# Query planes laid out to meet the high keys twice, fewer transfers per pair of heads, and a reordered start, in a fused attention and gated-MLP kernel

## The chip, the cores and the metric

One core of one Trainium2 chip. The metric is the device time of one execution in microseconds (us), as the median of several runs. Engines: PE (TensorE), DVE (VectorE), ACT (ScalarE), POOL (GpSimd) and SP (SyncE, which here only issues transfers).

## The reference

Windowed attention with a few sink keys, then a two-matrix network with a gate; all in float32, the weights come as float64. In short:

```python
# q, k, v: (4, 8, 768, 64); n_sink = 4, window = 128
scores = scale * np.matmul(q, k.transpose(0, 1, 3, 2))
keep = is_sink | in_window            # key < 4, or 0 <= row - key < 128
a = softmax(np.where(keep, scores, -1e9))
x = (a @ v) with heads side by side   # (4, 768, 512)
h = np.maximum(x @ w_in, 0.0)         # w_in (512, 1024)
conv = sum(conv_w[k] * shifted(h, k - 1) for k in range(3))   # along the rows
out = (h * sigmoid(conv)) @ w_out     # w_out (1024, 512)
```

## The kernel before

**Tiling.** Two heads share the 128 rows of the chip's memories: head 0 of a pair in rows 0 to 63, head 1 in rows 64 to 127. There are 16 pairs (four per batch), numbered g. A pair has six query tiles of 128; a tile meets its own 128 keys, the 128 before, and the 4 sinks (`KW` = 132 columns per key tile, the last 4 a copy of the sinks). One *step* is one query tile of one pair; `banded` (L451) walks 96 steps, 24 per batch, and fills the PE's time between them with pieces of the MLP of earlier rows (`Moe.unit`, L180). All engines run their own queues in program order; a scheduler that builds the program orders each queue by priorities and its own idea of time, and semaphores join them.

**Batch 0** (`prep32`, L349) scores in plain float32: q and k are transposed on PE (L357), ACT evacuates them (L288), q once per head with the other head's rows multiplied by zero (`headscale`).

**Batches 1 to 3** (`prep`, L295) split every float32 into a high and a low part of a shorter format and need three products: high q with high k, low q with high k, high q with low k. `turn_k` (L316) transposes a half of k, ACT casts it to two planes of `kk` (L334), DVE makes the low part in a scratch tile `bk` (L337), SP moves that to planes 2 and 3 (L340), ACT spreads the sinks over all four planes (L342), and two more transfers copy each head's high keys into the other head's rows (L344, L345). The other halves of planes 2 and 3 are zero; the first use of each `kk` copies them from a zeroed tile (L326). `turn_q` (L302) transposes, evacuates to scratch `bq` (ACT L288, DVE L310), and four transfers per half put high q in a head's own rows and low q in the other head's rows of `X` (L313, L314). `scores` (L372) then makes two products per head: X with plane j (high q on high k, low q on high k: L381), X with plane 2 + j (high q on low k, low q on zeros: L382). That is 8 + 4 + 2 transfers of this kind per pair, beside two loads each of q and k and one of v.

**The start.** SP loads the first halves of q and k of pairs 0 and 1 (L871), a flag is computed from `n_sink` and `window` (L874 to L876), and all engines branch on it (L906). After the branch DVE builds the mask tiles `w1`, `w2` (L473 to L478) and their minima `m1`, `m2` (`narrow_masks`, L489), POOL zeroes `A.zeros` and `c.vs` (the sink values of batch 0, in a spare part of `kks`), SP loads v of pair 0, the first weight tile, and the raw q and k of pair 2 into the slots that pair 0's transposes free.

**Weights.** Sixteen tiles of float64 and one of conv taps are converted, one per step from step 2 on (`WHEN`): ACT one pass (L118), DVE three and a subtraction (L121, L122, L123, L131), POOL one (L130).

**Sinks of later batches** (`sink_fetch`, `sink_split`) are loaded at the first step of a batch and split 3 steps later, by ACT and DVE on 12 rows (L440 to L443), then moved to `vsr` by four transfers (L446, L448).

Of the kernel before, what the change touches and what calls it, by code (L numbers as in the profile page):

```python
# [10 lines left out]
F32 = mybir.dt.float32  # L11
# [24 lines left out]
AHEAD = 200  # L36

# [236 lines left out]
class Attn:  # L274


    def __init__(self, c, x, kw, mp, mps):
# [6 lines left out]
        self.zeros = None  # L284
# [4 lines left out]

    def pieces_of(self, name, dtype):  # L290

        both = self.mp.tile([P, 512, 2], dtype, tag="nat", name=f"b{name}", bufs=3).rearrange("p n w -> p (n w)")
        return [both[:, 3 * P * x:3 * P * x + 3 * P].rearrange("p (t k) -> p t k", t=3) for x in range(2)]

    def prep(self, g, s, ahead=lambda: None):  # L295
# [6 lines left out]
        def turn_q(half):  # L302
# [4 lines left out]
            X = s.X[half] = ap.tile([P, 2, HTL, P], F32R, tag="X", name=f"X{g}{half}", bufs=3)  # L307
            H, L = self.pieces_of(f"q{g}{half}", F32R)
            self.evac(H, pt, -1.0 / math.sqrt(D))
            c.emptied = [nc.vector.scalar_tensor_tensor(out=L, in0=pt, scalar=-1.0 / math.sqrt(D), in1=f(H), op0=ALU.mult, op1=ALU.subtract)]  # L310
            for j in range(2):
                r, o = (slice(D * x, D * x + D) for x in (j, 1 - j))
                nc.sync.dma_start(f(X[r, j]), f(H[r]))  # L313
                nc.sync.dma_start(f(X[o, j]), f(L[r]))  # L314

        def turn_k(half):  # L316
            if half == 0:
                if g % 2 not in self.KK:
                    self.KK[g % 2] = ap.tile([P, 4, T, kw], F32R, tag="kk", name=f"kk{g}")
                    for j in range(2):  # L320
                        r = slice(D - D * j, P - D * j)
                        plane = f(self.KK[g % 2][r, 2 + j]).rearrange("p t k -> p (t k)")
                        if self.zeros is None:
                            nc.gpsimd.memset(plane, 0.0)
                        else:
                            nc.sync.dma_start(plane, self.zeros[r])  # L326
                s.kk = self.KK[g % 2]
            kk = s.kk[:, :, HTL * half:HTL * half + HTL, 0:P]
# [4 lines left out]
            for j in range(2):  # L333
                nc.scalar.copy(kk[:, j], pt)  # L334
            if half == 0:
                s.low = self.pieces_of(f"k{g}", F32R)
            c.emptied = [nc.vector.tensor_tensor(out=s.low[half], in0=pt, in1=f(kk[:, 0]), op=ALU.subtract)]  # L337
            for j in range(2):
                r = slice(D * j, D * j + D)
# [602 lines left out]
```

## Time and profile before

| what | us |
|---|---|
| median of 3 runs | 474.92 (474.6 to 476.47) |
| the profiled execution, its own time | 473.48 |
| its span, first to last instruction | 471.8 |
| PE busy | 444.6 (94%) |
| DVE busy | 339.0 (72%) |
| ACT busy | 321.3 (68%) |
| POOL busy | 281.3 (60%) |
| span before the first transpose on PE | 6.9 |

A busy share is a mean over stages with different limits, and a PE instruction counts from its issue to its end though the next one overlaps it. So the stages are read one by one: the start, the first batch with the conversion of the weights (to about 90 us), the change from batch 0 to batch 1 (about 104 to 126 us), and the long rest.

### The profile page before, as it was taken

What the parts mean: (1) busy time and instruction counts of PE and PEld (TensorE: products, weight loads), DVE (VectorE), ACT (ScalarE), POOL (GpSimd) and SP (SyncE); (2) the same over time, 40 slices, a digit from 0 to 9 for tenths busy, and PEclk for the clock granted to TensorE, in tenths of its full rate; (3) what the DMA queues carried; (4) which work ended last, traced back from release to release, by engine and by line L of the source; (5) the groups of instructions that cost most, each with busy time, mean ns of one, the idle gap of its engine ahead of it and who ended that gap; (6) DMA issues with size and microseconds to landing.
All of it is one profiled execution on the core that took longest, in us unless ns stands there. A gap on an engine that the chain in (4) does not pass through costs nothing.

```text
span 471.8 us, 10560 instructions
## 1 busy us (share of the span) xinstructions
PE 444.6 (94%) x3181; PEld 388.3 (82%) x3181; DVE 339.0 (72%) x1190; ACT 321.3 (68%) x1027; POOL 281.3 (60%) x557
## 2 busy tenths in 40 slices
PE   3898989898899999999999999999999999999994
PEld 3576768697798988898989898988989898998982
DVE  4799999758858668786766859685767663665562
ACT  4989957768867868785867767675857654554542
POOL 3474786626858658676755757667656671445340
PEclk9999999999999999999999999999999999999998
DMA  6888674388667472655273655545250101000001
GB/s 140 219 229 251 183 201 107 81 199 203 167 153 179 137 175 68 161 146 133 61 192 81 166 119 134 143 120 124 71 141 15 46 1 46 0 23 24 24 24 53
DMA packets 105851, 55.91 MB, mean 119 GB/s; under 512 B 83072, under 2 KB 98712, under 8 KB 105784
## 3 DMA queue, kind: packets, MB, share of 16 engines
q1 hardware_dynamic: 105640, 55.00, 45.5%
q8 instruction: 28, 0.46, 0.4%
q14 instruction: 39, 0.32, 0.2%
q10 hardware_dynamic: 144, 0.13, 0.1%
HBM read 28.17 MB, written 6.29 MB: 73 GB/s over the span
## 4 chain that ended last, share of the span: by engine, by line
PE 75%; DVE 11%; ACT 4%; POOL 3%; DMA 2%; issue 2%; DVEq 0%; POOLq 0%; ACTq 0%
PE ph L204 26%; PE po L239 25%; PE px L655 7%; PE sc L382 3%; PE sc L381 3%; PE pts L617 3%; PE px L678 2%; DVE stm L122 2%; PE tq L305 1%; PE tk L331 1%; DVE stm L123 1%; DMA kk<-bk 1%; DMA raw<-in_q_dram 1%; DVE roomH L577 1%; DVE roomL L577 1%
## 5 line engine op out<-in xcount | busy, mean ns | idle before, releaser
L239 PE MATMUL po<-woH,g 128*128 128x512 f32 x384 | 138.2, 405 | 1.5 <-POOL g L226 0.8
L204 PE MATMUL ph<-xH,wiH 128*128 128x258 f32 (+1 forms) x384 | 110.7, 288 | 0.0
L204 PE MATMUL ph<-xL,wiH 128*128 128x258 f32 (+1 forms) x384 | 109.6, 286 | 0.0
L204 PE MATMUL ph<-xH,wiL 128*128 128x258 f32 (+1 forms) x384 | 109.1, 284 | 0.0
L226 POOL TENSOR_SCALAR g<-t 128x256 fp32r<-128x256 f32 x94 | 44.3, 472 | 74.5 <-DVE t L219 50.6
L586 POOL TENSOR_SCALAR pe<-pe,sm 128x132 f32<-128x132 f32 (+1 forms) x144 | 62.8, 447 | 37.7 <-DVE sm L584 19.2
L239 PEld LDWEIGHTS po<-woH,g 128*128 128x128 f32 x384 | 69.4, 189 | 13.2 <-POOL g L226 1.7
L227 POOL TENSOR_TENSOR g<-t,g 128x256 fp32r<-128x256 f32 x94 | 74.5, 793 | 5.8
L239 PE MATMUL po<-woL,g 128*128 128x512 f32 x192 | 76.1, 396 | 0.0
L216 DVE SCALAR_TENSOR_TENSOR t<-hb,cw,t 128x256 f32<-128x256 f32 x96 | 53.8, 560 | 29.4 <-ACT t L215 28.9
L204 PEld LDWEIGHTS ph<-xH,wiL 128*128 128x128 f32 x384 | 72.8, 190 | 2.2
L204 PEld LDWEIGHTS ph<-xH,wiH 128*128 128x128 f32 x384 | 72.7, 189 | 2.0
L204 PEld LDWEIGHTS ph<-xL,wiH 128*128 128x128 f32 x384 | 72.7, 189 | 1.6
L580 ACT ACTIVATE pe<-pe,sm 128x132 f32<-128x132 f32 (+1 forms) x144 | 58.2, 406 | 14.4 <-DVE sm L577 12.8
L218 ACT ACTIVATE t<-t 128x256 f32<-128x256 f32 x96 | 40.1, 418 | 36.3 <-DVE t L217 35.9
L219 DVE SCALAR_TENSOR_TENSOR t<-t,hb 128x256 f32<-128x256 f32 x96 | 48.3, 504 | 15.1 <-ACT t L218 14.3
L215 ACT ACTIVATE t<-hb,cw 128x256 f32<-128x256 f32 x96 | 49.0, 511 | 12.4 <-POOL g L227 10.1
L217 DVE SCALAR_TENSOR_TENSOR t<-hb,cw,t 128x256 f32<-128x256 f32 x96 | 54.4, 567 | 4.0 <-POOL pe L586 0.5
L211 ACT ACTIVATE hb<-ph 128x258 f32<-128x258 f32 (+1 forms) x96 | 36.8, 384 | 17.4 <-PE ph L204 13.9
L577 DVE CUSTOM_DVE_ANT_0 pe<-sc,m 128x132 f32<-128x132 f32 (+1 forms) x144 | 39.8, 287 | 7.7 <-PE sc L382 6.9
L381 PE MATMUL sc<-kk,X 128*128 128x260 f32 (+1 forms) x144 | 42.3, 304 | 1.5 <-issue 1.1
L655 PE MATMUL px<-pT,vraw 128*64 128x128 f32 (+1 forms) x512 | 43.0, 317 | 0.0
(161 smaller groups left out, 896.1 us busy)
## 6 DMA issues: line engine op xcount, KB each, us to landing
X<-bq SPq DMA_DIRECT2D x96, 96.0 KB
vraw<-in_v_dram SPq DMA_DIRECT2D x16, 384.0 KB
out_dram<-stm SPq DMA_DIRECT2D x23, 256.0 KB
kk<-kk SPq DMA_DIRECT2D x24, 198.0 KB
raw<-in_k_dram SPq DMA_DIRECT2D x24, 192.0 KB
raw<-in_q_dram SPq DMA_DIRECT2D x24, 192.0 KB
kk<-bk SPq DMA_DIRECT2D x48, 96.0 KB
raw<-in_q_dram SPq DMA_DIRECT2D x16, 96.0 KB
```

Source lines behind the costliest of these rows:

```text
L204: self.latest = nc.tensor.matmul(u.h[:, 0:W], w[:, cc, ff * P:(ff + 1) * P], x[:, cc, t0:t1], start=(i == 0), stop=(i == len(prods) - 1))
L215: nc.scalar.mul(a, prev, cw[:, 0, ff:ff + 1])
L216: nc.vector.scalar_tensor_tensor(out=e, in0=this, scalar=cw[:, 1, ff:ff + 1], in1=a, op0=ALU.mult, op1=ALU.add)
L217: nc.vector.scalar_tensor_tensor(out=a, in0=nxt, scalar=cw[:, 2, ff:ff + 1], in1=e, op0=ALU.mult, op1=ALU.add)
L219: nc.vector.scalar_tensor_tensor(out=a, in0=e, scalar=1.0, in1=this, op0=ALU.add, op1=ALU.mult)
L227: nc.gpsimd.tensor_tensor(out=u.g[:, 1], in0=a, in1=f(u.g[:, 0]), op=ALU.subtract)
L239: ins = nc.tensor.matmul(po[:, 0:c.DM], u.g[:, a, tt * P:(tt + 1) * P], w[:, ff, :], start=(ff == 0 and i == 0), stop=(ff == NFF - 1 and i ...
L381: self.c.pin(self.nc.tensor.matmul(pc, X[:, j, u, :], kk[:, j, lo:hi], start=True, stop=False))
L577: nc.vector.tensor_tensor_reduce(out=pe[:, j, cols], in0=pc[:, P - at:SW][:, cols], in1=mk, op0=ALU.add, op1=ALU.min, scale=1.0, scalar=3. ...
L580: exp = nc.scalar.activation(pe[:, j, cols], pe[:, j, cols], AF.Exp, bias=sm[:, j:j + 1], scale=-1.0, accum_out=sm[:, 2 + 2 * j:3 + 2 * j])
L586: nc.gpsimd.tensor_scalar(pe[:, j, cols], pe[:, j, cols], sm[:, 8 + j:9 + j], 1.0, ALU.mult, ALU.mult)
L655: ins = nc.tensor.matmul(px[h][D * j:D * j + D, P * at:P * at + n], s.v[:, j, kt, :], pT, start=(h not in open_), stop=False, skip_group_c ...
```

## The change

- **q.** `X` has four planes. ACT evacuates q twice per half with `headscale`, so plane j holds high q of head j in its own rows and zeros in the other's; DVE makes plane 2 + j, the low part, zero in the other's rows. Then one transfer per head copies high q into the other head's rows of plane j.
- **k.** `kk` has two planes. The low part goes to a scratch tile `low`; after the second half one transfer per head moves it into the other head's rows of plane j. ACT spreads the sinks over two planes after the first half, POOL spreads them over `low`. No zero planes are left.
- **Products.** High q on both halves of the rows meets high keys in one half and low keys in the other; low q meets the same plane. Still two products per head and tile. Per pair 4 + 2 transfers stay of 14.
- **Start.** k of pairs 0 and 1 is loaded by ACT's queue; v of pair 0 before the branch. PE makes 8 products of zeros before the branch (`WAKE`), one after pair 0's q transposes and 3 after its k transposes (`IDLE`). One of the two evacuations of pair 0's q moves from ACT to DVE; the masks wait for it, their minima for step 21. The zeroed tiles and the batch 0 sink values live elsewhere.
- **Sinks** of batch 1 are fetched at step 21 instead of 24, and split at 24.

```diff
+WAKE = 8
+IDLE = {"q": 1, "k": 3}
         def turn_q(half):
...
-            H, L = self.pieces_of(f"q{g}{half}", F32R)
-            self.evac(H, pt, -1.0 / math.sqrt(D))
-            c.emptied = [nc.vector.scalar_tensor_tensor(out=L, in0=pt, scalar=-1.0 / math.sqrt(D), in1=f(H), op0=ALU.mult, op1=ALU.subtract)]
+            X = s.X[half] = ap.tile([P, 4, HTL, P], F32R, tag="X", name=f"X{g}{half}", bufs=3)
+            c.emptied = []
+            for j in range(2):
+                self.evac(X[:, j], pt, c.headscale[:, j:j + 1])
+                c.emptied.append(nc.vector.scalar_tensor_tensor(out=X[:, 2 + j], in0=pt, scalar=c.headscale[:, j:j + 1], in1=f(X[:, j]),
+                                                                op0=ALU.mult, op1=ALU.subtract))
             for j in range(2):
                 r, o = (slice(D * x, D * x + D) for x in (j, 1 - j))
-                nc.sync.dma_start(f(X[r, j]), f(H[r]))
-                nc.sync.dma_start(f(X[o, j]), f(L[r]))
+                nc.sync.dma_start(f(X[o, j]), f(X[r, j]))
         def turn_k(half):
...
-                nc.sync.dma_start(f(kk[r, 2 + j]), f(s.low[half][r]))
-            if half and kw > P:
-                nc.scalar.copy(s.kk[:, :, :, P:kw], f(s.kk[:, :, 0:1, 0:kw - P]).to_broadcast([P, 4, T, kw - P]))
+            if half == 0 and kw > P:
+                nc.scalar.copy(s.kk[:, :, :, P:kw], f(s.kk[:, :, 0:1, 0:kw - P]).to_broadcast([P, 2, T, kw - P]))
+                nc.gpsimd.tensor_copy(s.low[:, :, P:kw], f(s.low[:, 0:1, 0:kw - P]).to_broadcast([P, T, kw - P]))
             if half:
-                nc.sync.dma_start(f(s.kk[D:P, 0]), f(s.kk[0:D, 0]))
-                nc.sync.dma_start(f(s.kk[0:D, 1]), f(s.kk[D:P, 1]))
+                for j in range(2):
+                    r, o = (slice(D * x, D * x + D) for x in (j, 1 - j))
+                    nc.sync.dma_start(f(s.kk[o, j]), f(s.low[r]))
@@ prep32, pair 0 only
+                    ins = nc.tensor.matmul(c.spare, still[:, 0:P], still[:, 0:P], start=True, stop=True)
+                    if g == half == 0 and j:
+                        c.moved = nc.vector.tensor_scalar(s.X[half][:, j], pt, c.headscale[:, j:j + 1], None, ALU.mult)
@@ scores
-            self.c.pin(self.nc.tensor.matmul(pc, X[:, j, u, :], kk[:, 2 + j, lo:hi], start=False, stop=True))
+            self.c.pin(self.nc.tensor.matmul(pc, X[:, 2 + j, u, :], kk[:, j, lo:hi], start=False, stop=True))
@@ banded
-            nc.vector.tensor_tensor(out=mk[:, NS:KW], in0=w[:, 0:P], in1=w[:, KW:SW], op=ALU.min)
+            ins = nc.vector.tensor_tensor(out=mk[:, NS:KW], in0=w[:, 0:P], in1=w[:, KW:SW], op=ALU.min)
+            follow(c, ins, c.turned, "late")
...
+    follow(c, nc.vector.tensor_scalar(w1[:, KW:SW], inw, -NEG, NEG, ALU.mult, ALU.add), c.moved, "masks later")
...
-            if t == 0 and g and g % NPAIR == 0:
-                sinks = sink_fetch(c, m, g // NPAIR)
+            if i == NSTB - 3 or t == 0 and g > NPAIR and g % NPAIR == 0:
+                sinks = sink_fetch(c, m, max(1, g // NPAIR))
@@ attention_gated_mlp
+        for i in range(WAKE):
+            nc.tensor.matmul(turn, still[:, 0:P], still, start=True, stop=True)
     for i in range(RAWB):
-        load_half(c, i // 2, "qk"[i % 2], 0, c.raw[i])
+        load_half(c, i // 2, "qk"[i % 2], 0, c.raw[i], nc.scalar if i % 2 else nc.sync)
+    load_v(c, 0, 0, 0, T // 2)
```

How it moves instructions, at three places. First SP's queue behind the branch, before (`raw_67` and `raw_68` are the slots for raw q and k, `vraw_69` and `vraw_70` those for v, `wi_0r` the first weight tile):

```order
L401 DMA vraw_69<-in_v_dram 128x3x64 x2
L106 DMA wi_0r<-in_moe_w_in_dram 128x1024
L401 DMA raw_67<-in_q_dram 128x3x64 x2
L401 DMA raw_67<-in_k_dram 128x3x64 x2
L106 DMA wi_1r<-in_moe_w_in_dram 128x1024
L401 DMA raw_68<-in_q_dram 128x3x64
```

and now:

```order
L108 DMA wi_0r<-in_moe_w_in_dram 128x1024
L108 DMA wi_1r<-in_moe_w_in_dram 128x1024
L400 DMA raw_67<-in_q_dram 128x3x64 x2
L400 DMA vraw_70<-in_v_dram 128x3x64
L400 DMA raw_67<-in_k_dram 128x3x64 x2
L108 DMA wi_2r<-in_moe_w_in_dram 128x1024
```

The first two weight tiles now stand ahead of the third pair's q, one tile did before. Second, DVE's queue from the branch to the first weight tile, before (`m_147` is the mask of a first tile, `roomH` and `roomL` hold masks and scores of batch 0, `sc` are scores in the accumulators, `sm` row minima):

```order
L475 TENSOR_TENSOR roomH<-vraw_70 128x4
L471 TENSOR_SCALAR m_147<-m_147 128x128
L489 TENSOR_TENSOR m_148<-roomH 128x128
L476 TENSOR_SCALAR roomH<-roomH 128x4
L477 COPY roomH<-roomH 128x260
L478 TENSOR_SCALAR roomH<-vraw_70 128x4
L489 TENSOR_TENSOR m_149<-roomH 128x128
L577 ISA roomH,sm_163<-sc_0_0_208,m_147 128x128
```

and now:

```order
L472 TENSOR_SCALAR m_163<-m_163 128x128
L357 TENSOR_SCALAR X_192<-trq_187,headscale 128x384
L706 TENSOR_SCALAR roomL<-vraw_70 128x128
L707 TENSOR_SCALAR roomL<-vraw_70 128x128
L708 TENSOR_TENSOR roomL<-vraw_70 128x4
L709 TENSOR_SCALAR roomL<-roomL 128x4
L710 COPY roomL<-roomL 128x260
L711 TENSOR_SCALAR roomL<-vraw_70 128x4
L570 ISA roomH,sm_172<-sc_0_0_228,m_163 128x128
```

The evacuation of q stands ahead of the masks, and the two minima have gone from here. Third, SP's queue for the second pair of batch 1, before (`kk_1392` are its keys, `X_1470` and `X_1528` its two halves of q, `kk_1140` the keys of the pair after):

```order
L326 DMA kk_1392<-roomH 64x792 x2
L398 DMA vraw_70<-in_v_dram 128x12x64
L340 DMA kk_1392<-bk_1401 64x3x128 x4
L401 DMA raw_68<-in_q_dram 128x6x64
L313 DMA X_1470<-bq_1471 64x384
L314 DMA X_1470<-bq_1471 64x384
L313 DMA X_1470<-bq_1471 64x384
L314 DMA X_1470<-bq_1471 64x384
L344 DMA kk_1392<-kk_1392 64x792
L345 DMA kk_1392<-kk_1392 64x792
L313 DMA X_1528<-bq_1529 64x384 x2
L314 DMA X_1528<-bq_1529 64x384 x2
```

and now:

```order
L334 DMA kk_1413<-low_1414 64x792 x2
L397 DMA vraw_70<-in_v_dram 128x12x64
L311 DMA X_1486<-X_1486 64x384
L400 DMA raw_68<-in_q_dram 128x6x64
L311 DMA X_1486<-X_1486 64x384
L400 DMA raw_68<-in_q_dram 128x6x64
L311 DMA X_1543<-X_1543 64x384
```

Sixteen transfers of keys and queries stood there, six do now (the last one behind these rows); the four transfers into `vsr` (batch 1's sinks), which stood behind them, now stand ahead.

## Rows read from the trace of the kernel before

**Rows 1.** The page's chain that ended last, by engine.

```profile
PE 75%; DVE 11%; ACT 4%; POOL 3%; DMA 2%; issue 2%; DVEq 0%; POOLq 0%; ACTq 0%
```

**Rows 2.** Busy time by stage: window, its length, then PE, PEld, DVE, ACT, POOL, clock, DMA.

```profile
7.00:15.00 8.00, 7.03 (x25) 5.49 (x26) 3.90 (x22) 5.71 (x17) 3.43 (x11) 1.00 0.87 222
25.00:90.00 65.00, 57.82 (x432) 46.75 (x431) 62.98 (x182) 51.03 (x153) 43.25 (x62) 1.00 0.64 174
90.00:110.00 20.00, 20.00 (x175) 18.26 (x174) 12.81 (x50) 15.48 (x49) 7.23 (x15) 1.00 0.85 203
110.00:126.00 16.00, 13.07 (x87) 11.10 (x87) 13.24 (x64) 12.50 (x49) 12.94 (x26) 1.00 0.63 163
160.00:400.00 240.00, 239.70 (x1760) 213.00 (x1759) 171.74 (x652) 166.97 (x564) 156.72 (x320) 1.00 0.43 107
```

**Rows 3.** Timeline of the start: start, length, engine, line, what, idle before and its releaser.

```profile
6.91 0.88 PE L357 MATMUL trq<-ident,raw 128*128 128x128 f32 x3 [6.91 <-SPq L938]
...
7.68 0.42 SPq L106 DMA_DIRECT2D wi_0r<-in_moe_w_in_dram  x1
...
7.90 1.05 ACT L288 ACTIVATE X<-trq,headscale 128x384 f32<-128x384 f32 x2 [1.93 <-DVE roomH L474]
...
8.27 0.90 SPq L401 DMA_DIRECT2D raw<-in_q_dram  x2
...
9.01 0.90 PE L357 MATMUL trq<-ident,raw 128*128 128x128 f32 x3 [0.59 <-ACT X L288]
...
10.71 0.29 DVE L577 CUSTOM_DVE_ANT_0 roomH<-sc,m 128x128 f32<-128x128 f32 x1 [1.60 <-PE sc L378]
...
12.89 0.66 ACT L118 ACTIVATE stm<-wi_0r 128x512 f32<-128x512 f32 x1 [0.48 <-DMA wi_0r<-in_moe_w_in_dram]
...
13.60 0.88 PE L357 MATMUL trq<-ident,raw 128*128 128x128 f32 x3 [0.38 <-DMA kks<-in_v_dram]
...
13.69 0.41 DVE L121 TENSOR_SCALAR stm<-stm 128x512 int32<-128x512 int32 x1
...
15.44 0.49 PE L357 MATMUL trk<-ident,raw 128*128 128x128 f32 x3
...
15.67 0.69 DVE L122 SCALAR_TENSOR_TENSOR stm<-wi_0r,stm 128x512 int32<-128x512 int32 x1
```

**Rows 4.** Chain of waits in order of time, at the start.

```profile
8.27 4.86 DMA raw<-in_q_dram
```

**Rows 5.** Timeline of the change from batch 0 to batch 1: SP, PE, ACT, DVE.

```profile
106.18 3.02 SPq L340 DMA_DIRECT2D kk<-bk  x4
...
113.81 2.44 SPq L313 DMA_DIRECT2D X<-bq  x2
...
111.75 0.26 PE L637 MATMUL tk<-identr,sk 128*72 128x128 f32 x1 [0.67 <-DVE sk L629]
...
116.84 0.30 PE L381 MATMUL sc<-kk,X 128*128 128x128 f32 x1 [1.05 <-issue]
...
122.69 0.36 PE L381 MATMUL sc<-kk,X 128*128 128x260 f32 x1 [0.40 <-PE sc L382]
...
123.97 0.41 PE L617 MATMUL pts<-ident,pe 128*128 128x128 f32 x2 [0.80 <-ACT pT L619]
...
123.28 0.27 ACT L342 CAST kk<-kk 128x96 fp32r<-128x96 f32 x1 [1.60 <-DMA kk<-bk]
...
109.58 0.67 DVE L441 TENSOR_TENSOR sink<-sink 12x512 fp32r<-12x512 f32 x1
```

**Rows 6.** Groups by line and form: busy us, mean ns, idle before.

```profile
L310 DVE SCALAR_TENSOR_TENSOR bq<-tq,bq 128x384 fp32r<-128x384 f32 x24 | 13.2, 552 | 4.0 <-ACT bq L288 3.9
...
L489 DVE TENSOR_TENSOR m<-roomH 128x128 f32<-128x128 f32 x2 | 0.6, 288 | 0.0
...
L288 ACT ACTIVATE bq<-tq 128x384 fp32r<-128x384 f32 x24 | 11.9, 496 | 2.4 <-PE tq L305 2.1 <-issue 0.3
...
L342 ACT CAST kk<-kk 128x96 fp32r<-128x96 f32 x12 | 3.3, 273 | 4.2 <-DMA kk<-bk 4.2
```

More of the change, by code (lines that the diff above doesn't have):

```diff
@@ L318, in turn_k @@
                 if g % 2 not in self.KK:
[L319 to L326, printed above, removed]
+                    self.KK[g % 2] = ap.tile([P, 2, T, kw], F32R, tag="kk", name=f"kk{g}")
                 s.kk = self.KK[g % 2]
-            kk = s.kk[:, :, HTL * half:HTL * half + HTL, 0:P]
+                low = self.mp.tile([P, 512, 2], F32R, tag="nat", name=f"low{g}", bufs=3).rearrange("p n w -> p (n w)")
+                s.low = low[:, 0:T * kw].rearrange("p (t k) -> p t k", t=T)
+            tiles = slice(HTL * half, HTL * half + HTL)
             pt = self.mps.tile([P, HTL, P], F32, tag="h", name=f"tk{g}{half}", bufs=3)
@@ L356, in turn @@
             for t in range(HTL):
-                c.pin(nc.tensor.transpose(pt[:, t, :], s.raw[nm, half][:, t].rearrange("p a d -> p (a d)"), c.ident))
+                turned = c.pin(nc.tensor.transpose(pt[:, t, :], s.raw[nm, half][:, t].rearrange("p a d -> p (a d)"), c.ident))
+            if g == half == 0:
+                still = c.v_raw[0][:, 0, HTL:T].rearrange("p t d -> p (t d)")
+                for i in range(IDLE[nm]):
+                    ins = nc.tensor.matmul(c.spare, still[:, 0:P], still[:, 0:P], start=True, stop=True)
+                    follow(c, ins, turned, "in its place")
+                    turned = ins
             if nm == "q":
-                s.X[half] = f(self.ap.tile([P, 2, HTL, P], F32R, tag="X", name=f"X{g}{half}", bufs=3))
+                s.X[half] = f(self.ap.tile([P, 4, HTL, P], F32R, tag="X", name=f"X{g}{half}", bufs=3))
                 for j in range(2):
-                    self.evac(s.X[half][:, j], pt, c.headscale[:, j:j + 1])
+                    if g == half == 0 and j:
+                        c.moved = nc.vector.tensor_scalar(s.X[half][:, j], pt, c.headscale[:, j:j + 1], None, ALU.mult)
+                    else:
+                        self.evac(s.X[half][:, j], pt, c.headscale[:, j:j + 1])
             else:
@@ L460, in banded @@
     ap, ps = A.ap, A.ps
[L465 removed]
+    n0, n1 = T * KW, 3 * NPAIR * P
+    half_row = n1 // 2
+    wide = [m.room[1][:, n:n + SW] for n in (6 * SW + n0, 7 * SW + n0)]
     m0 = cp.tile([P, P], F32, name="m0")
@@ L511, in banded @@
                             base=-2 * NS, channel_multiplier=1)
+    pts = ps.tile([P, 2, 2, P], F32, name="pts")
+    c.spare = pts[:, 0, 0]
     m.weights()
@@ L547, in fetch @@
             asked[0] += 1
-    pts = ps.tile([P, 2, 2, P], F32, name="pts")
     def scores(g, t):
@@ L712, in banded @@
         x()
-    load_v(c, 0, 0, 0, T // 2)
+    follow(c, nc.vector.tensor_scalar(w1[:, KW:SW], inw, -NEG, NEG, ALU.mult, ALU.add), c.moved, "masks later")
+    follow(c, nc.vector.tensor_scalar(w1[:, 0:P], prv, -NEG, NEG, ALU.mult, ALU.add), c.moved, "masks later")
+    follow(c, nc.vector.tensor_tensor(out=w1[:, P:KW], in0=sk[:, 0:NS], in1=prv[:, 0:NS], op=ALU.is_gt), c.moved, "masks later")
+    follow(c, nc.vector.tensor_scalar(w1[:, P:KW], w1[:, P:KW], -NEG, NEG, ALU.mult, ALU.add), c.moved, "masks later")
+    follow(c, nc.vector.tensor_copy(w2, w1), c.moved, "masks later")
+    masks = nc.vector.tensor_scalar(w2[:, P:KW], sk[:, 0:NS], -NEG, NEG, ALU.mult, ALU.add)
+    afterwards(nc.gpsimd.memset(zeros, 0.0))
+    afterwards(nc.gpsimd.memset(two, 0.0))
+    afterwards(nc.gpsimd.memset(third, 0.0))
     m.fetch(1)
```

51 lines of the change are left out of this document (19 added, 32 removed).

## The prediction

> **What bounds the kernel now.** The chain of waits comes first: three quarters of it are PE, and most of the rest DVE, ACT and POOL [rows 1]. The busy times by stage say where the rest lies [rows 2]. From 160 to 400 us PE is idle for 0.30 us of 240: nothing but less work on PE could shorten that stretch, and the change takes no product away there. Three places are left. From 25 to 90 us, while the weights are converted, DVE is busy for 62.98 of 65 us: DVE is the bound, and PE is idle for 7.2 us. From 90 to 110 us PE works off what has piled up and is never idle. From 110 to 126 us, where batch 1 takes over, PE is idle for 2.93 us. And before 15 us the stage is short of everything: DVE is busy for only 3.90 of 8 us.
>
> So a gain must come from an earlier start of the stretch that DVE bounds, or from the waits at the change of batches. What is gained there stays, since behind each PE or DVE works without a pause.
>
> The sum is made against the profiled execution, 473.48 us; the median of the three runs shown, 474.92, lies 1.44 above it, and I take the same for the changed kernel.
>
> **The start, -2.0.** What DVE leaves idle from 7 to 15 us is 8.00 - 3.90 = 4.10 us [rows 2]. The evacuation of q that moves to it costs one 128x384 pass from the accumulators, 0.55 us by its nearest row [rows 6], so at most 3.5 us can be won; at least nothing. In between I add what the rows let me name [rows 3]:
> - ACT makes the two evacuations of pair 0's q one after the other, 1.05 us; with one on DVE, half of that, 0.5 us, leaves the way to the first scores, for which DVE stands idle 1.60 us. The masks, 1.4 us of small passes that fill DVE's time before, now come after that evacuation and still fit in the wait.
> - The three transposes at 6.91 and at 9.01 us take 0.88 and 0.90 us, the same three at 15.44 only 0.49. The clock column prints 1.00 from the start [rows 2], but these durations say that PE ran at the lower of its two levels (1.2 GHz) until about 14 us, and at the higher one (2.4 GHz) after it had been busy for most of the 8 us before. Zero products before the branch and in the gaps are meant for that. Two lots of transposes at the higher level would save 0.4 us each. I take half, 0.4 us, with 0 and 0.8 as the ends.
> - The first weight tile is now asked for right behind the branch, about 1 us sooner than at 7.68, and v of pair 0 no longer stands ahead of it. ACT waited for its landing until 12.89. If its first two passes on DVE (0.41 at 13.69 and 0.69 at 15.67) are done in the idle time instead, 1.1 us leaves the stretch behind.
>
> What I give nothing for is the third pair's q. It was asked for at 8.27 and released PE 4.86 us later [rows 4], at 13.60. Now a second weight tile, 512 KB (128 x 512 numbers of 8 bytes), stands ahead of it, and PE's next scores stand behind its transposes. It may come as late as before.
>
> The Trainium skill speaks against the zero products: "TensorE: Matmul & The Clock Gate", section "What's actually happening", says that the slow clock is the default and that idleness brings it back, and its section "Part 4" that transposes do not count as activity in the same way. The products before the branch end some microseconds before the first transpose. By that rule their 0.4 us falls away, and the sum would end at 471.5 instead of 471.1; that a busy stretch raises the clock is as the rows of 6.91 and 15.44 show it.
>
> The products themselves cost nothing: eight run before the branch, when PE has nothing to do for 6.91 us, and four lie in gaps such as the 0.59 us before 9.01 [rows 3]. If that cover were gone they would cost their own length, about 0.3 us each by the transposes at the lower level.
>
> **The change of batches, -2.4.** PE's four waits between 110 and 126 us are 0.67, 1.05, 0.40 and 0.80 us, 2.92 in all [rows 5], and each has an address in the change.
> - 1.05 us at 116.84 ("issue"): the first scores of the second pair wait for transfers that SP was late to issue. Four of `kk<-bk` took SP 3.02 us and two of `X<-bq` 2.44 us, and sixteen stood in that row. Six are left.
> - 0.40 and 0.80 us: ACT stood 1.60 us before its spread of the sinks, because that needs the low keys to have landed; copies that PE needs were queued behind it. The spread now takes only what ACT itself wrote. Over the kernel that wait is 4.2 us [rows 6]; elsewhere PE does not feel it.
> - 0.67 us at 111.75: DVE was late with a small subtraction because the split of the sinks (0.67 us and two more passes) came in between. It now runs three steps sooner, where DVE is idle for 7 us of 20 [rows 2].
>
> In their place come, for the first two pairs, four more evacuations on ACT at 0.50 us and four more passes on DVE at 0.55 [rows 6]. ACT is idle for 3.5 of these 16 us and DVE for 2.8, and 1.9 us of DVE's sinks leave, so they fit. I charge one of them, 0.5 us, as a lateness in front of something that PE needs. High q now leaves for the other half of the rows only after both DVE passes have read the zeros there, one pass later than before; the queries are asked for a step or more ahead, which hides it. Ends: 0 and -2.9.
>
> **The masks' minima, +0.6.** Two passes of 0.29 us [rows 6] were made at about 8 us in DVE's idle time; now they come at step 21, in the stretch where DVE has no time to spare [rows 2]. Ends: 0 (they stand behind the last weight tile, where DVE is past its worst) and +0.6.
>
> **The steady pairs, 0.** Each pair costs two more evacuations and two more DVE passes: for twelve pairs 24 x 0.496 = 11.9 us on ACT and 24 x 0.552 = 13.2 us on DVE [rows 6]. Against that stand 73 us of idle time on ACT and 68 on DVE in the 240 us [rows 2]. POOL's copy of the sinks is small (nearest row 0.27 us [rows 6]) beside 83 us of idle time, and SP issues eight transfers less per pair. The price is nothing as long as no late evacuation meets a product that PE is about to start; from below, PE's idle time there, 0.30 us, is all that could be won; from above see the rivals.
>
> **Sum.** -2.0 - 2.4 + 0.6 = -3.8: 473.48 becomes 469.7 in a profiled execution, and 474.92 becomes **471.1** in the median.
>
> **The rivals.**
> - *Everything goes.* The start gives its full 3.5, the change of batches 2.9, the minima cost nothing, and with the weight tiles sooner on the spot a quarter of PE's 7.2 us of idle time before 90 us goes too, 1.8: -8.2, so 466.7. For it: DVE's queue holds the first weight's passes sooner. Against it: DVE has no time left in that stage, and nothing of its work goes.
> - *Nothing to measure.* The second weight tile, 512 KB, at the 222 GB/s of that stretch [rows 2] delays the third pair's q by 2.3 us; that eats the start, and the added evacuations eat half of the other gain: -1.2 + 0.6 = -0.6, so 474.3. For it: PE waited on exactly this transfer [rows 4]. The case in which the zero products do not do what they are for lies here too.
> - *Slower.* The added ACT and DVE passes come in bursts, in front of the copies and exponentials that feed PE. If each half of a pair makes PE wait for one evacuation, 0.50 us, that is 1.0 us per pair, and for eleven pairs +11; with the -3.8, +7.2, so 482.1. It decides from 0.6 us per pair on, (3.8 + 2.4) / 11, where 2.4 us is the 0.5% that a measurement of this kernel can tell from no change. Against it: PE is idle for 0.30 us in ten such pairs now, with ACT busy for 70% of the time; ACT rises to about 75%.
>
> **How the numbers follow.** The forecast 0.50, everything goes 0.15, nothing to measure 0.22, slower 0.13. The forecast's own ends are 474.92 - 3.5 - 2.9 = 468.5 and 474.92 + 0.6 = 475.5. The range takes most of the better rival and the whole of the third: 465.8 to 475.8; left out are the slower case and the best edge. Faster by over 0.5% (under 472.5): the better rival and nine tenths of the forecast, 0.60. Slower by over 0.5%: the slower case, 0.13. The rest, 0.27, is no change.
>
> **What would show it.** Right: DVE's idle time from 7 to 15 us falls to about 2 us and the transposes at 9 us take near 0.5; the stretch of full DVE ends about 2 us sooner; between 105 and 125 us PE has no wait of a microsecond, and ACT's spread of the sinks waits for no transfer. Wrong: the third transposes of q come after 13.6 us, or PE shows new waits on ACT's evacuations of q in every pair from 130 us on; either would put the time at or above 474.

## The result, and the profile after

The changed kernel takes 478.52 us (median of 6, 477.64 to 479.33), the kernel before 474.76 in the same sitting: ratio 1.0084, interval [1.0057, 1.0112]. It is slower by 3.8 us by the medians and 4.0 by the ratio, where 3.8 less were forecast. The profiled execution took 477.64 (span 475.9) against 473.48. Here and below, changes by the ratio are taken against the kernel before of the same sitting, and the medians of e14 and e16 leave out one far slower execution each (1523 and 878 us).

The stages, the same windows as [rows 2]:

```profile
7.00:15.00 8.00, 5.90 (x39) 4.67 (x40) 5.38 (x23) 5.71 (x17) 3.85 (x18) 1.00 0.93 268
25.00:90.00 65.00, 60.05 (x431) 47.22 (x430) 60.18 (x178) 50.21 (x149) 42.81 (x60) 0.97 0.57 159
90.00:110.00 20.00, 19.47 (x165) 17.39 (x164) 15.64 (x55) 16.74 (x52) 9.12 (x20) 1.00 0.68 163
110.00:126.00 16.00, 15.02 (x108) 13.67 (x107) 13.50 (x59) 13.54 (x50) 12.07 (x27) 1.00 0.39 107
160.00:400.00 240.00, 236.77 (x1729) 208.29 (x1728) 176.92 (x667) 173.53 (x573) 159.01 (x328) 1.00 0.31 78
```

Much of the forecast is there. DVE's idle time from 7 to 15 us fell from 4.10 to 2.62, and PE's from 110 to 126 us from 2.93 to 0.98. But from 160 to 400 us PE is idle for 3.23 us instead of 0.30. Who it waited for there (the waits of PE in that window):

```profile
PE po L241 <- POOL g L228: 2.3, 4, 0.7
PE ph L206 <- ACT hb L213: 0.4, 2, 0.3
PE sc L379 <- PE pts L610: 0.4, 1, 0.4
```

`g` is the MLP's gate output, `po` the second MLP product that reads it. One such place, from the timeline of the changed kernel:

```profile
164.01 0.58 ACT L289 ACTIVATE X<-tq,headscale 128x384 fp32r<-128x384 f32 x1
...
164.56 0.41 DVE L221 SCALAR_TENSOR_TENSOR t<-t,hb 128x256 f32<-128x256 f32 x1
...
165.07 0.57 POOL L228 TENSOR_SCALAR g<-t 128x256 fp32r<-128x256 f32 x1 [1.12 <-DVE t L221]
...
165.69 0.49 PE L241 MATMUL po<-woH,g 128*128 128x512 f32 x1 [0.67 <-POOL g L228]
```

An evacuation of q stands right there, and so the rival "slower" looked proved. It was not. The tanh (L220) that `g` depends on had left ACT at 163.74, before that evacuation began; what came between, on DVE, was a pass of the next unit's gate and softmax work. And the runs show that the wait stays without the added passes (e17).

**A ledger.** Idle time misses what PE loses between products that overlap. So for each profiled run I summed, product by product, the usual time from one start to the next (a mean per kind from the kernel before, the longest tenth left out, idle products not counted; 402.7 us in all). The lag is the time of a product minus that sum. These sums are mine; no view of the profile prints them:

```
work done   before  changed  e1     e3     e13    e15    e17
 30 us       29.14   34.17   36.40  29.91  29.87  35.92  35.40
 50 us       39.18   39.38   41.60  39.94  39.90  41.11  40.59
100 us       48.02   46.47   49.39  49.55  47.83  48.14  47.10
380 us       62.00   65.35   64.64  68.29  63.80  66.91  65.36
100 to 380   13.98   18.88   15.25  18.74  15.97  18.77  18.26
```

Against the kernel before, the changed one loses 5.0 us by a work of 30 (some 64 us into the span), has won nearly all of it back at 50, wins 1.75 more at the change of batches, and then loses 4.9 over batches 1 to 3.

Not all of this is equally firm. With the products sorted into kinds by tiles and shape, the changed kernel is 4.1 us behind at 30, 4.5 behind at 50, 1.1 ahead at 100 and 3.4 behind at 380: the early figures depend on the kinds, the 1.1 to 1.6 us won by 100 and the 4.5 to 4.9 lost behind it do not. Part of the early differences is PE's clock: before 40 us the profile's clock column shows one stretch at the lower level in the changed kernel, e15 and e17, two in e1 and none in the kernel before, e3 and e13. From a work of 100 to 380 it shows none in any of the seven.

### The profile page after: what moved, and what is told of

Read it like the earlier page. It is cut to its first block, busy times and chain, and to the rows that moved or that the text cites. A ratio compares the mean times of both kernels' runs of the same rounds, so it can differ in the third digit from the quotient of the medians.

```text
span 475.9 us, 10494 instructions
## 1 busy us (share of the span) xinstructions
PE 451.3 (95%) x3205; PEld 391.4 (82%) x3205; DVE 349.6 (73%) x1216; ACT 333.6 (70%) x1050; POOL 284.6 (60%) x570
## 4 chain that ended last, share of the span: by engine, by line
PE 70%; DVE 12%; ACT 6%; POOL 5%; issue 2%; DMA 2%; POOLq 0%; DVEq 0%; SPq 0%; ACTq 0%
PE ph L206 24%; PE po L241 24%; PE px L648 8%; PE pts L610 3%; PE sc L380 3%; PE sc L379 3%; PE px L671 2%; PE tq L301 1%; POOL g L228 1%; DVE t L218 1%; ACT X L289 1%; POOL roomL L579 1%; PE tk L323 1%; DVE stm L124 1%; DVE stm L125 1%
## 5 line engine op out<-in xcount | busy, mean ns | idle before, releaser
L218 DVE SCALAR_TENSOR_TENSOR t<-hb,cw,t 128x256 f32<-128x256 f32 x96 | 54.5, 567 | 34.8 <-ACT t L217 34.6
L220 ACT ACTIVATE t<-t 128x256 f32<-128x256 f32 x96 | 40.2, 419 | 32.0 <-DVE t L219 31.5
L221 DVE SCALAR_TENSOR_TENSOR t<-t,hb 128x256 f32<-128x256 f32 x96 | 46.0, 479 | 15.8 <-ACT t L220 14.9
L219 DVE SCALAR_TENSOR_TENSOR t<-hb,cw,t 128x256 f32<-128x256 f32 x96 | 52.1, 542 | 4.0
L569 DVE COPY_PREDICATED sc<-before,sc 128x128 f32<-128x128 int32 x120 | 33.6, 289 | 17.6 <-PE sc L380 16.9
L648 PE MATMUL px<-pT,vraw 128*64 128x128 f32 (+1 forms) x512 | 44.3, 320 | 0.5 <-ACT pT L598 0.5
```

The lines of the kernel that those rows point to most:

```text
L218: nc.vector.scalar_tensor_tensor(out=e, in0=this, scalar=cw[:, 1, ff:ff + 1], in1=a, op0=ALU.mult, op1=ALU.add)
L219: nc.vector.scalar_tensor_tensor(out=a, in0=nxt, scalar=cw[:, 2, ff:ff + 1], in1=e, op0=ALU.mult, op1=ALU.add)
L221: nc.vector.scalar_tensor_tensor(out=a, in0=e, scalar=1.0, in1=this, op0=ALU.add, op1=ALU.mult)
L648: ins = nc.tensor.matmul(px[h][D * j:D * j + D, P * at:P * at + n], s.v[:, j, kt, :], pT, start=(h not in open_), stop=False, skip_group_c ...
```

## The experiments

First theories: **A**, the added passes make PE wait in the steady pairs; **C**, the new start loses; **B**, later called **O**: the scheduler orders every queue anew for each build, and that order makes the difference.

**e1: the new start alone**, on the kernel before:

```diff
... (in words)
+WAKE, IDLE, loads of k on nc.scalar, v ahead of the branch, c.moved on DVE, masks and minima after it
 X, kk, sinks as before
```

> Kernel before, with the whole new start (idle products, k loads on ACT's queue, v before the branch, one evacuation of pair 0's q on DVE, masks and minima later) and the old planes and sinks. Theory C (the start loses): the weights come 2 to 6 us earlier but the softmax of batch 0 and the first MLP product about 4 us later, as in the changed kernel, and without the cheaper change of batches nothing gives it back: +3 to +5 us over before, ratio 1.006 to 1.010. Rival R (the start is worth what was forecast, and the whole loss is the new planes'): -2 us, ratio 0.996. In between, 0.999 to 1.003, the delay of batch 0 is swallowed at the change of batches whatever the planes are.

475.21 us, ratio 1.0012 [0.9988, 1.0036]: nothing won, nothing lost that the runs can tell. The traces suggest why. The last weight's subtraction and the last exponential of batch 0, in the kernel before, the changed one and e1:

```profile
86.62 0.68 DVE L131 TENSOR_TENSOR woL<-stm,woH 128x512 fp32r<-128x512 f32 x1
...
91.97 0.50 ACT L580 ACTIVATE roomL<-roomL,sm 128x260 f32<-128x260 f32 x1
```

```profile
82.95 0.69 DVE L133 TENSOR_TENSOR woL<-stm,woH 128x512 fp32r<-128x512 f32 x1
...
96.77 0.50 ACT L573 ACTIVATE roomL<-roomL,sm 128x260 f32<-128x260 f32 x1
```

```profile
85.17 0.69 DVE L133 TENSOR_TENSOR woL<-stm,woH 128x512 fp32r<-128x512 f32 x1
...
98.90 0.50 ACT L585 ACTIVATE roomL<-roomL,sm 128x260 f32<-128x260 f32 x1
```

The weights end 3.7 us sooner in the changed kernel and batch 0's softmax 4.8 us later; in e1 it is 1.5 sooner and 6.9 later. DVE and ACT did the one before the other.

**e2: the new planes and the earlier sinks, old start.**

```diff
... (in words)
-WAKE, IDLE, c.moved, loads on nc.scalar, v ahead of the branch
 X, kk, sinks as changed
```

> Changed kernel with the old start: new planes of q and k and the earlier sinks alone. Theory C with A (the start loses about 4; the planes gain about 3 us of waits at the change of batches and lose about 3 us in the steady pairs): 0 over before, ratio 0.997 to 1.003, PE idle about 3 us from 160 to 400 us and about 1 us from 105 to 130 us. Rival R: +5 to +6 us, ratio 1.011 or more. If the steady loss is only an order that the scheduler chose because the weights came earlier, PE idle from 160 to 400 us stays under 1 us and the ratio is 0.993.

484.83 us, 1.0203 [1.0161, 1.0244]: 10 us over before. Rival R had the direction (1.011 or more), but gave 5 to 6 us, and e1 had just shown the start to be worth nothing by itself. The parts, 0.7 and 10, don't add up to the whole, 3.8.

**e3: the passes alone**, on the kernel before:

```diff
+            self.evac(L, pt, -1.0 / math.sqrt(D))
             self.evac(H, pt, -1.0 / math.sqrt(D))
+            nc.vector.scalar_tensor_tensor(out=L, in0=pt, scalar=..., in1=f(H), ...)
             c.emptied = [nc.vector.scalar_tensor_tensor(out=L, ...
```

> Kernel before, and for each half of q one more ACT evacuation and one more DVE subtraction that write a scratch tile again (the result is unchanged): the added passes without the new planes. Theory A (added passes in front of the gate's passes make PE wait): PE idle 3 us or more from 160 to 400 us instead of 0.30, and +3 to +5 us, ratio 1.006 to 1.010. Theory B (the passes are hidden, the loss comes from the order or from where the transfers lie): 0 to +1 us, ratio under 1.002.

480.50 us, 1.0133 [1.0094, 1.0172], 18.74 us lost from 100 to 380, and PE idle for 3.5 us from 160 to 400 us. It speaks for A, but this build's queues were ordered anew too.

**e4: no idle products**, on the changed kernel:

```diff
-WAKE = 8
-IDLE = {"q": 1, "k": 3}
```

> Changed kernel without the eight products before the branch and the four in the gaps. Theory D (the early high clock brings the fall back at 25.75 us, 3.4 us at the lower level, and delays batch 0): the clock stays up after it rises at about 15 us, and the time is 1 to 3 us shorter than the changed kernel's. Rival: the products save their 0.8 us at the start and the fall back costs nothing, since DVE is the bound there: 0 to 1 us longer than the changed kernel.

483.84 us, 1.0203 [1.0165, 1.0241]: 5.3 us over the changed kernel. Theory D falls.

**e5: only the eight before the branch away**, every queue otherwise the same:

```diff
-WAKE = 8
+WAKE = 0
```

> Changed kernel with no products before the branch and the four in the gaps kept: every other instruction stands in the same place of its queue. Theory D (the early rise of the clock brings the fall back at 25.75 us, which costs up to 1.7 us): 0.5 to 2 us shorter than the changed kernel, 476.5 to 478. Rival (the early rise is worth what the transposes lose at the lower level): 0.5 to 1.5 us longer. If it comes near the 483.8 of the changed kernel without any idle product, the eight products and not the order of the first 100 us made that difference.

478.56 us, 1.0077 [1.0052, 1.0102]: the eight are worth nothing in the median. So either the four in the gaps or e4's other order made 5.3 us.

**e6 and e7: one of the two passes of e3 alone.**

```diff
+            self.evac(L, pt, -1.0 / math.sqrt(D))                                # e6
+            nc.vector.scalar_tensor_tensor(out=L, in0=pt, ..., in1=f(H), ...)    # e7
```

> Kernel before with one more ACT evacuation per half of q (a scratch tile written twice), nothing more on DVE. Load theory: both passes together made before 6 us longer, some 5 of it over the twelve pairs of batches 1 to 3. If ACT is what the gate waits for, this one gives 3 us or more (ratio 1.006 to 1.010); if DVE is, 0 to 1.5 us (under 1.003).

479.91 us, 1.0099 [1.0064, 1.0135].

> Kernel before with one more DVE subtraction per half of q, nothing more on ACT. If DVE is what the gate and the softmax wait for, 3 us or more (ratio 1.006 to 1.010); if ACT is, 0 to 1.5 us. If each alone gives under 1.5 us, only their sum in one burst makes PE wait.

479.04 us, 1.0100 [1.0060, 1.0141]. Each alone costs most of what both cost (4.7 and 4.7 us against 6.3 by the ratios): if it were the load alone, one would expect less.

**e8: the second product one unit later**, on the changed kernel, with some buffers moved to make room (the same move as in e11 below):

```diff
-TRAIL = 2
+TRAIL = 3
...
```

> Changed kernel in which the second MLP product of a unit runs three units behind the first, instead of two, with one more buffer for the gate's output (and the sink values of batch 0 in another place, to make room). Load theory: the waits of PE for the gate's output (2.3 of the 4.5 us of PE's waits from 90 to 400 us) go, and some of the 4.9 us that the steady pairs lost with them: 2 to 4 us shorter than the changed kernel, 474.5 to 476.5. Rival (the loss is PE's waits for scores and softmax, or the order): within 1 us of it, or longer, since the first MLP output comes one unit later in batch 0.

486.44 us, 1.0259 [1.0223, 1.0294], a miss: PE waited longer for the gate from 90 to 400 us (4.2 us against 2.3), and the start was later too. Most of the loss is not TRAIL's: e11 has the same move of buffers and no more, and e8 is 1.9 us over it by the medians, 3.7 by the ratios.

**e9 and e10: one cast of k less per half**, plane 1 by a transfer, on the changed kernel and on the kernel before. e9's edit is shown; e10's is its like on four planes, with the spread of the sinks in two parts:

```diff
-            for j in range(2):
-                nc.scalar.copy(s.kk[:, j, tiles, 0:P], pt)
+            nc.scalar.copy(s.kk[:, 0, tiles, 0:P], pt)
...
+                nc.sync.dma_start(f(s.kk[D:P, 1]), f(s.kk[D:P, 0]))
```

> Changed kernel with one cast of k on ACT per half instead of two: plane 1's own rows are copied from plane 0 by one more transfer per pair, ahead of the low keys' transfers. ACT then makes as many evacuations per pair as in the kernel before, DVE still one per half of q more. Load theory (one more ACT pass per half cost before 5 us, one more DVE pass 4): 2 to 3 us shorter than the changed kernel, 475.5 to 476.5, its lag in the steady pairs near that of the DVE pass alone. Rival (the loss is the burst behind q's transposes, not the sum of ACT's work): within 1 us of the changed kernel. If the longer chain of transfers makes the queries wait: longer.

478.48 us, 1.0069 [1.0041, 1.0096]: no gain over the changed kernel.

> Kernel before with one cast of k on ACT per half instead of two, plane 1 by one more transfer per pair, and the spread of the sinks in two parts. ACT makes 0.65 us less per pair. Load theory, taken downwards: 1 to 2 us shorter than before, ratio 0.996 to 0.998. Rival (PE had no idle time left in the steady pairs, so nothing to win): 0, or longer by what the longer chain of transfers costs at the change of batches, 0 to 2 us.

481.37 us, 1.0138 [1.0107, 1.0169]: less work on ACT, and as slow as with more.

**e11: hardly anything but another order**, on the changed kernel:

```diff
-    half_row = n1 // 2
+    half_row = n1 // 4
...
-    third = cp.tile([6 * SP, NPAIR * P], F32, name="vs2")
+    third = m.room[1][0:6 * SP, 8 * SW + n1 // 4:8 * SW + n1 // 4 + NPAIR * P]
...
-                for x in range(0, 2 * half_row, half_row):
+                for x in range(0, 4 * half_row, half_row):
```

> Changed kernel with the third row of batch 0's sink values in another place and the zeros for the later sinks copied by four transfers instead of two: no work added or taken away, but the scheduler orders the first 100 us otherwise (326 of 786 places in PE's first tenth); from there on all queues are the same. If such shifts of order decide by themselves: 2 to 5 us off the changed kernel in either direction, as the version without idle products was (+5.3). If not: within 1 us of it.

484.56 us, 1.0182 [1.0151, 1.0213]: by the ratios 4.6 us, by the medians 6.0 over the changed kernel. PE, DVE, ACT and POOL have as many instructions as in the changed kernel, SP two small transfers more; but a tile now shares a buffer with others, so that a wait on that buffer can have its part beside the order. (PE's queue is the same again only from 195 us on in the changed kernel, not from 100 us.)

**e12: all but the planes.**

```diff
 as e1, and
-            if t == 0 and g and g % NPAIR == 0:
+            if i == NSTB - 3 or t == 0 and g > NPAIR and g % NPAIR == 0:
```

> Kernel before with the new start and the earlier sinks, old planes: everything of the change but the planes. Load theory: the new planes' passes cost 4 to 5 us, so this is 0 to 1 us from before (ratio 0.998 to 1.002), with about 1 us less of waits at the change of batches. If the forecast was right for the start and the sinks and only the planes were mis-sized: 2 to 3 us shorter than before, ratio 0.994 to 0.996.

482.75 us, 1.0150 [1.0113, 1.0187]: 7.5 over e1 by the medians, 6.5 by the ratios, for sinks fetched three steps sooner.

From here on the order was held. A table gives, for each engine, the order of another build; each instruction follows the one before it by an edge that sets the order of issue and waits for nothing:

```diff
+        for a, b in zip(seq, seq[1:]):
+            c.tc.add_manual_dep(b, a.name, DependencyInfo(DependencyClass.NoSync, ...), reason="order")
```

**e13: e3's passes in the order of the kernel before.**

> Kernel before with one more ACT and one more DVE pass per half of q, as in the run that made it 6 us longer, but every queue kept in the order of the kernel before (issue-order edges from each instruction to the next on its engine, which wait for nothing else), the added passes beside the ones they repeat. Theory O (the scheduler's new order makes the loss): 0 to 1.5 us over before, ratio 1.000 to 1.003. Theory L (the passes make it, in whatever order): 4 to 6 us, ratio 1.008 to 1.013.

477.94 us, 1.0084 [1.0060, 1.0107]; the profiled execution, 475.53, lags by 1.8 more than before at its end, but it is the second fastest of six (475.34 to 479.08). Just inside L by the median, near O by the profile: the passes cost something here, between 1.8 and 4.2 us. The kernel before with the edges and no edit was not run, so what the edges themselves cost is not known; e15 below, with the edges and twelve products less, is 0.7 to 1.4 us over the changed kernel.

**e14: the planes in the order of the kernel before.**

> The new planes of q and k alone (old start, sinks at step 24), with every queue in the order of the kernel before; a new pass stands beside the one that it adds to, POOL's copy of the sinks where DVE's low half was ready. Theory O: the planes are worth what was forecast, about 2 us shorter than before at the change of batches and nothing in the steady pairs, ratio 0.994 to 0.999. Theory L: the steady pairs lose 4 to 5 us, which the change of batches gives back in part: ratio 1.004 to 1.008.

488.00 us, 1.0295 [1.0277, 1.0313]: worse than either theory. `px` now waited for the low queries' passes (PE px L665 <- DVE X L307: 3.8 us from 90 to 400 us), which I had put side by side. An order made for other work does not fit; this run does not price the planes.

**e15: e4 in the order of the changed kernel.**

> Changed kernel without any idle product, every queue in the order of the changed kernel (without that the same kernel was 5.3 us longer than the changed one). Theory O: the products are worth nothing, as the eight before the branch were (478.56 against 478.52), so 478 to 479.5. Rival (the four in the gaps keep the clock up): 481 to 484.

479.19 us, 1.0113 [1.0093, 1.0134]. The same instructions took 483.84 in their own order: 4.3 us (by the ratios) to 4.65 (by the medians) are the order. All twelve idle products together are worth 0.7 to 1.4, if the edges cost nothing.

**e16: e10 in the order of the kernel before.**

> Kernel before with one cast of k on ACT per half instead of two and one transfer more per pair, every queue in the order of the kernel before. With the order made anew it was 6.6 us longer. Theory O: all of that was the order, so 0 or up to 1.5 us shorter than before, ratio 0.997 to 1.000. If the longer chain of transfers makes the queries wait: 1 to 3 us longer.

485.95 us, 1.0237 [1.0207, 1.0267]. The longer chain of transfers costs much of it, at the change of batches: `sc` waits 4.6 us in one piece (PE's waits, 90 to 140 us):

```profile
PE sc L382 <- issue: 4.6, 1, 4.6
PE sc L382 <- DMA X<-bq: 1.3, 1, 1.3
```

So e10 does not speak against A as I had read it: its extra transfer has a price of its own.

**e17: half the passes, in the order of the changed kernel.** ACT and DVE make as many passes per half of q as before the change. To leave PE's products as they are, the kernel makes the second head's scores from the first head's queries, and leaves out the transfer of the second head's high q.

```diff
-            for j in range(2):
+            for j in range(1):
                 self.evac(X[:, j], pt, c.headscale[:, j:j + 1])
...
-            for j in range(2):
+            for j in range(1):
                 r, o = (slice(D * x, D * x + D) for x in (j, 1 - j))
...
-            ... matmul(pc, X[:, j, u, :], ...), matmul(pc, X[:, 2 + j, u, :], ...)
+            ... matmul(pc, X[:, 0, u, :], ...), matmul(pc, X[:, 2, u, :], ...)
```

> Changed kernel, every queue in the order of the changed kernel, with one ACT evacuation and one DVE subtraction per half of q instead of two, and the transfer of the second head's high q left out: the second head's scores are made from the first head's queries, with the same products on PE. ACT and DVE then make as many passes per half of q as in the kernel before. Theory L (the passes make the loss): 4 to 5 us shorter than the changed kernel, 473.5 to 474.5, at or below the kernel before. Theory O (the order makes it): within 1 us of the changed kernel, 477.5 to 479.5. Both: in between, 475 to 477.

477.48 us, 1.0050 [1.0026, 1.0073]: 1.0 us less than the changed kernel by the medians, 1.6 by the ratios. By the medians that is theory O (within 1 us), by the ratios it is "both"; it is not L, which gave 4 to 5. PE's groups from 160 to 400 us in the changed kernel, in e17, in e13 and in the kernel before (line, what, count, busy, mean ns, idle before):

```profile
L241 PE MATMUL po<-woH,g 128*128 128x512 f32 x217 | 78.5, 405 | 2.3 <-POOL g L228 2.3
```

```profile
L241 PE MATMUL po<-woH,g 128*128 128x512 f32 x217 | 78.5, 405 | 2.5 <-POOL g L228 2.5
```

```profile
L239 PE MATMUL po<-woH,g 128*128 128x512 f32 x223 | 79.3, 404 | 0.9 <-POOL g L226 0.9
```

```profile
L239 PE MATMUL po<-woH,g 128*128 128x512 f32 x223 | 79.4, 405 | 0.3 <-POOL g L226 0.3
```

and the load of the stage in e17:

```profile
160.00:400.00 240.00, 236.94 (x1734) 208.82 (x1734) 169.65 (x652) 166.88 (x559) 159.20 (x329) 1.00 0.28 72
```

DVE (169.65) and ACT (166.88) are no busier than before the change [rows 2], yet the waits stay: they come before the same four units' products, 0.67, 0.40, 0.84 and 0.63 us here and 0.67, 0.74, 0.23 and 0.64 in the changed kernel. The one shown above, in e17:

```profile
166.30 0.50 PE L241 MATMUL po<-woH,g 128*128 128x512 f32 x1 [0.67 <-POOL g L228]
```

Where the passes were added to the old order, these waits grew only from 0.3 to 0.9 us.

**e18: the earlier sinks alone, in the order of the kernel before.**

> Kernel before with batch 1's sinks fetched and split three steps sooner, every queue in the order of the kernel before but for these eleven instructions. Forecast of the change's sinks: the wait of 0.67 us at 111.75 goes, and what DVE is relieved of behind it: 0.5 to 1 us shorter than before, ratio 0.998 to 0.999. Theory O: the 7 us that the sinks seemed to cost beside the new start (482.75 against 475.21) were the order made anew, so no loss here. Rival (the earlier split meets the last weights and batch 0's softmax): 1 to 3 us longer.

478.32 us, 1.0083 [1.0055, 1.0111]: the rival's direction, and with 4.3 us (3.9 by the ratio) more than the 1 to 3 it gave. The sinks' eleven instructions stand in their new place. SP's queue in e18:

```profile
103.36 1.81 SPq L446 DMA_DIRECT2D vsr<-sink  x2
...
107.70 0.81 SPq L448 DMA_DIRECT2D vsr<-vsr  x1
...
109.11 2.77 SPq L340 DMA_DIRECT2D kk<-bk  x4
111.92 0.82 SPq L448 DMA_DIRECT2D vsr<-vsr  x1
...
116.86 0.55 SPq L344 DMA_DIRECT2D kk<-kk  x1
```

and what PE waited for, 105 to 126 us:

```profile
PE sc L381 <- DMA kk<-kk: 3.1, 1, 3.1
```

The sinks' transfers now stand ahead of the keys', which SP reaches at 109.11 instead of 106.18 [rows 5]. So the earlier place of the sinks costs something with the old planes. How much is less clear: of the profiled execution's lag on the kernel before, 1.3 us is there ahead of the sinks (the 25th `po` by `woH`, at 97.64 us there), and it is 2.5 from the 49th (134.15 us) on: 1.2 us at the change of batches.

**e12 against e18: one work, two orders.** In batches 1 to 3 both have exactly the instructions of the kernel before: the old planes, no added pass. e12 has an order of its own there, e18 the old one. From 160 to 400 us, e12 and then e18:

```profile
160.00:400.00 240.00, 236.97 (x1728) 208.75 (x1727) 169.03 (x655) 165.78 (x565) 157.55 (x322) 0.99 0.42 105
```

```profile
160.00:400.00 240.00, 239.70 (x1760) 212.86 (x1759) 172.36 (x658) 167.75 (x569) 158.03 (x322) 1.00 0.43 107
```

PE is idle for 3.03 us in e12 and 0.30 in e18, with DVE and ACT no busier. The changed kernel's 3.23 can thus come about with no added pass and no new plane. (One stretch of e12 near 190 us ran at the lower clock.)

No version was faster than the kernel before.

## Why the prediction was wrong

**The steady pairs: forecast 0, measured +4.9 (lag from 100 to 380). This step failed.** It weighed the added passes against idle time and took for granted that everything else would stay in its place. The scheduler rebuilt every queue. By whose order a kernel has, the loss from 100 to 380 sorts itself:

```
order of the kernel before   before 13.98   e18 14.00   e13 (passes added) 15.97   e16 16.08
order of the changed kernel  changed 18.88  e5 18.75    e15 18.77                  e17 (passes halved) 18.26
```

Taking the passes away gives 0.6 of the 4.9 back; adding them to the old order costs 2.0. The rest, 2.9 to 4.3 us, goes with the order. That an order by itself makes such a loss in the steady pairs is shown by e12 against e18, and that one costs 4.3 to 4.65 us of a whole execution by e4 against e15. That nothing else of the change has a part in the 4.9 is not shown: e17 still has the new planes of k, with POOL's copies and the new transfers, though none of PE's waits from 160 to 400 us is for a transfer. And the table has only kernels whose order was made for nearly their own work. e14, in the order of the kernel before too, does not belong to its row: it took 14 us more, with PE waiting for passes that stood too late.

How the order does it: over the MLP units from 130 to 330 us I took the time from the end of a unit's last `ph` to its gate output, and from there to the first `po` that reads it. Before: 6.46 and 2.41 us. Changed: 5.97 and 1.68. The gate is ready *sooner* in the changed kernel, on busier engines; but the new queue of PE asks for it 1.2 us sooner still (8.87 against 7.65 in all). In e17 it is 5.81 and 1.79, with the same waits; in e13, with the passes in the old order, 6.91 and 2.12. That the shorter distance is how, is read from these sums and not tested by a run. Which decision of the scheduler made it is open.

Neither sign of being wrong came that the prediction had named: the third pair's q was transposed at 12.81 us, and no wait of PE from 90 to 400 us names an evacuation of q. It had no sign for an order made anew.

**The rival "slower"** had the right sign and place. Its price was one evacuation per half, 1.0 us per pair, and it was to decide from 0.6 on. The passes cost 1.0 to 1.6 us for all twelve pairs in the new order (e17) and 1.8 to 4.2 in the old (e13), under 0.4 per pair. In the changed kernel, which has the new order, they are the smaller part of the cause; e13's median leaves room for more in the old one.

**The start: forecast -2.0, measured 0** (e1: ratio 1.0012, or -0.6 to +1.7 us). Its steps came true: one evacuation on DVE, the third pair's q at 12.81 instead of 13.60, the weights' stretch 3.7 us shorter. What failed is the sentence "What is gained there stays, since behind each PE or DVE works without a pause". DVE was full because two kinds of work shared it; the weights went first and batch 0's softmax, which ends that stage, came 4.8 us later. The 0.4 us for the clock is not there in the median either: the eight products before the branch are worth nothing (e5), all twelve 0.7 to 1.4 us (e15), and that interval overlaps the changed kernel's.

**The change of batches: forecast -2.4 and +0.6 for the minima, measured -1.4 to -1.75** (PE's idle time from 90 to 126 us, 2.93 before and 1.51 now; the lag from 50 to 100). This term mostly held: the four waits [rows 5] are gone, and from 105 to 126 us one of 0.9 us, for `hb`, is all that came in their place. The minima ran at 88.3 us, behind the last weight tile, the low end that the prediction named. One reason in it was wrong. Fetching the sinks sooner is no gain by itself: with the old planes e18 is 4.3 us over the kernel before. That it did no harm here may be because six transfers of keys and queries per pair stand on SP instead of fourteen; no run tests that.

So up to 100 us of work the sum had the sign and less than half of its size (forecast -3.8, measured -1.1 to -1.6), and behind it the loss of 4.5 to 4.9 us turned it round.

Open stays why e13's median is 4.2 over before and its profiled execution lags by only 1.8, what the edges cost by themselves, what the new planes of k cost, and how the planes would do in an order made for them by hand.

## What to carry to other kernels

Where a scheduler orders the queues, an edit is two edits: the work, and a new order. Time a nearly neutral edit first: here it moved the time by 4.6 to 6.0 us, more than any term of the forecast. Then hold the order by issue edges and change the work alone, and time the edges with no edit too. An order held for work it does not fit prices nothing (e14). And when a stage is "bound by an engine", ask which of the works on that engine ends the stage.

## What was not expected of the hardware

The clock rose early, as meant. PE's timeline of the changed kernel, the products before the branch and the first transposes:

```profile
1.18 4.86 PE L876 MATMUL turn<-vraw 128*128 128x192 f32 x16 [1.18 <-DVE vraw L872]
7.12 0.52 PE L346 MATMUL trq<-ident,raw 128*128 128x128 f32 x3 [1.08 <-SPq L946]
```

The eight products, sixteen instructions, took 0.61 us each where I had put 0.3, but nothing else ran on PE then. The three transposes behind them took 0.52 us instead of 0.88 [rows 3]: the pause was 1.08 us, not some microseconds, and did not bring the lower level back. The Trainium skill ("TensorE: Matmul & The Clock Gate", section "What's actually happening") says that idleness brings the slow clock back. At this pause it did not.

But the higher level did not stay. The stretch from 25 to 30 us in the changed kernel, and in e5, which has the same queues without the eight early products:

```profile
25.00:30.00 5.00, 5.00 (x30) 3.11 (x29) 4.30 (x12) 1.75 (x7) 4.64 (x7) 0.66 0.80 252
```

```profile
25.00:30.00 5.00, 4.93 (x40) 3.49 (x38) 4.29 (x12) 3.29 (x11) 4.64 (x8) 1.00 0.75 247
```

In the first of the two PE ran part of the time at 1.2 GHz (granted clock 0.66) while its own record shows it busy throughout, waiting products included. These two executions took 477.64 and 475.60 us, and their lag differs by 0.8 us at a work of 30 and by 1.1 at PE's last product (469.23 against 468.17 us); the other 1.0 us lies behind PE's last product. So this one pair puts such a fall of the clock at about 1 us of an execution, if the eight products themselves cost nothing.
